# RWKV attention and SwiGLU block: scores and state products of a late unit in two shared banks, VectorE's small work handed out singly, one set of DMAs begun by ScalarE

## The chip, the core and the metric

The kernel runs on one core of one Trainium2 chip. The metric is the time of one execution in device microseconds (us); for the kernel before the change it is 601.09 us, the median of three runs (599.85 to 602.52). The engines are named as in the profile: PE is TensorE's matmul, PEld its weight load, DVE is VectorE, ACT is ScalarE, POOL is GpSimd, SP is the queue of SyncE, which only issues DMAs. A suffix q (SPq, ACTq) is the sequencer of an engine: it waits and issues, and the engine does no arithmetic in that time.

## The reference

An attention block with a decaying state (4 batches, 8 heads, 768 positions, head size 48) is followed by a gated feed-forward block over its 3072 rows of 384 numbers (inner size 1536). All is fp32.

```python
for t in range(S):                       # r, k, v: (4, 8, 768, 48); w, u: (8, 48)
    kt, vt, rt = (k[:, :, t], v[:, :, t], r[:, :, t])
    cur = np.einsum('bhd,bhe->bhde', u[None] * kt, vt)
    y[:, :, t] = np.einsum('bhd,bhde->bhe', rt, state + cur)
    state = w[None, :, :, None] * state + np.einsum('bhd,bhe->bhde', kt, vt)
x = y.transpose(0, 2, 1, 3).reshape(3072, 384)
g = x @ w_gate                           # (3072, 1536)
out = (g / (1 + np.exp(-g)) * (x @ w_val)) @ w_out
```

## The kernel before the change

**Units and steps.** Attention is cut into 24 units, and a loop over steps s = 4 ... 25 works on several units at once: in step s the kernel scales and loads for units s + 1 to s + 3, turns r and k of unit s, computes the scores of unit s - 1 and the outputs of unit s - 2. Units 0 to 11 hold 128 positions of one batch. Units 12 to 23 (those from `PAIRED` = 12 on, the late units) hold 64 positions of each of two batches, one on partitions 0 to 63 and one on 64 to 127; the index `p` names the half. All of the change is in the late units.

**One late unit.** For unit i these parts follow each other:
- `diagonal` (L376, ACT): eight small activations (one for each head) write the diagonal u·k·r terms into `own`, which lies in the tile `zs`. They are not issued at once but put into the queue `small`.
- `fill` (L503 and L504, SP): four DMAs fill the unit's coefficient tile `At`: two bring r from `rT`, two bring the diagonals from `zs`. `At` exists twice, and units take turns.
- `paired_scores` (L516, PE): 32 matmuls of `rT` and `kT` into two banks.
- `masked_copy` (L524, DVE): four predicated copies take the strictly causal scores out of these banks into `At`. Of the four, two are issued at once and two are put into the queue `lazy`.
- `paired_outputs` (L550, PE, then L554, ACT): 64 matmuls of `At` with v and the state (both in `v_ld`) into one bank, and ACT copies it into `xT`, the input of the feed-forward part.
- `paired_update` (L567, PE; L585, DVE; L589, POOL): 32 matmuls form k·v for the state into two banks, four DVE additions add them to the state in `v_ld`, two POOL multiplications apply the decay.

**Banks.** PSUM (the matmuls' output memory) has eight banks here. Four (`bank`) serve the feed-forward matmuls; a bank must be emptied (evicted) by ACT or DVE before the matmuls of a later piece may write it. The other four (`ring`) go round through `next_psum`: each call takes the next. One late step takes one for the outputs, two for the scores and two for the state products: five of a ring of four, so that the last state bank of a step is the bank in which the outputs of the same step lie.

**Pieces.** The feed-forward matmuls fill the time between the parts of attention. They lie in the list `todo` as pieces of one or a few matmul groups each. `feed(n, pops)` issues n pieces, and after each it takes one item of `lazy` and up to `pops` items of `small`. `gaps(s, n)` calls it at five places of a step; `turn_blocks` calls it once between its two DVE transposes (L456). The pieces that matter are of two kinds: in one (`three_beside`, L922) each bank is evicted by DVE additions and ACT copies (L946), followed by the silu (L953, ACT) and its product; in the other (`project`, L738) the sums of h (L711 to L715, DVE) are needed before the matmuls.

**Order.** Nothing is scheduled automatically: each engine runs its instructions in the order in which the program issues them, and waits on semaphores. In step s from 14 on that order was: `own_sum` and `diagonal(s)`, `gaps(s, 0)`, outputs of s - 2, the rest of `lazy`, scores of s - 1, two masked copies, state products, additions and multiplications of s - 2, loads of v, `gaps(s, 1)`, `turn_blocks(s)`, moves for the next turn (L435, SP), `gaps(s, 2)`, the rest of `small`, `fill(s)`, `gaps(s, 3)`, `gaps(s, 4)`. Steps 14 to 16 have 14 pieces each, steps 18 to 20, 22 and 23 have 10, step 17 has 4 and step 21 has 6.

**After the loop** the last four groups of the feed-forward part run by themselves (L922, L1151); the change leaves them as they are.

Of the kernel before, what the change touches and what calls it, by code (L numbers as in the profile page):

```python
# [15 lines left out]
P = 128  # L16
# [6 lines left out]
def fast(  # L23
# [474 lines left out]
    def fill(i):  # L498

        rT = turned[i][:].rearrange("p a (e t) -> p (a e) t", e=2)  # L500
        for p in range(2):
            there, here = slice(64 - 64 * p, P - 64 * p), slice(64 * p, 64 * p + 64)
            sp.dma_start(out=both(i)[there, p], in_=rT[there])  # L503
            sp.dma_start(out=both(i)[here, p], in_=own[here, i % 2])  # L504

    def paired_scores(i, ps):

        rT = turned.pop(i)[:].rearrange("p a (e t) -> p (a e) t", e=2)
        kt = kT[i % 2][:].rearrange("p a (e t) -> p (a e) t", e=2)
        ps = [x.rearrange("p a (e t) -> p (a e) t", e=2)[:, 0:HP] for x in ps]  # L510
# [18 lines left out]
        lazy.popleft()()  # L529
        lazy.popleft()()  # L530
# [25 lines left out]
    def paired_update(i):  # L556

        if i + 2 >= N:
            return
        ps = [next_psum(HP, D) for _ in range(2)]  # L560
        for n in range(HP):
            for p in range(2):
                rows = slice(64 * p, 64 * p + 64)
                for g in range(2):
# [6 lines left out]
                    )  # L571
        for p in range(2):
            o = 64 - 64 * p

            def state(a):
                x = v_ld[part(i, p)[0]][o : o + D, a, 0:1]
                return bass.AP(
                    tensor=x.tensor, offset=x.offset,
                    ap=[list(x.ap[0]), [VW, a.stop - a.start], [64, 2], [1, D]],
                )  # L580

            for g in range(2):
                x = 64 * (1 - (p ^ g))
                ze = state(slice(HP // 2 * g, HP // 2 * g + HP // 2))
                dve.tensor_add(  # L585
                    ze, ps[p][x : x + D].rearrange("p (a e) d -> p a e d", e=2), ze
                )
            ze = state(slice(0, HP))
            pool.tensor_mul(ze, ze, w64[o : o + D].unsqueeze(3).to_broadcast([D, HP, 2, D]))  # L589
# [33 lines left out]
    def update(i):  # L623
        if i >= PAIRED:
            paired_update(i)
            return
# [671 lines left out]
    def gaps(s, n):  # L1298

        if s not in EARLY:  # L1300
# [5 lines left out]
            feed(share[0] // 5 + (n < share[0] % 5) - (n == 1 and BLOCKS <= s < N))  # L1306
# [100 lines left out]
    for s in range(4, N + 2):  # L1407
# [31 lines left out]
        if 4 <= s - 1 < N:  # L1439
            if s <= PAIRED:  # L1440
                flush()
            if s - 2 >= PAIRED:
                outputs(s - 2)
            scores(s - 1)
            if LATE <= s < PAIRED + 2:
                outputs(s - 2)
            if s >= LATE:
                update(s - 2)
            if PAIRED <= s < N:
                load_v(s)  # L1450
            gaps(s, 1)
        if BLOCKS <= s < N:
            turn_blocks(s)
        if late:
# [17 lines left out]
        elif s < N:  # L1472
            flush()
            fill(s)
# [446 lines left out]
```

## Time and profile before

| | |
|---|---|
| median of three runs | 601.09 us |
| the profiled execution, its own time | 598.33 us |
| its span, first to last instruction | 596.6 us |
| TensorE clock granted | 0.998 of full speed |
| matmuls (PE) busy | 575.0 us, 5370 instructions |
| outputs L550, 768 matmuls | 13.3 us |
| scores L516, 384 matmuls | 8.3 us |
| state products L567, 320 matmuls | 8.5 us |
| diagonals L376, 96 activations | 29.0 us, 343 ns each |
| decay L589, 20 POOL multiplications | 16.5 us, 825 ns each |
| DMA At<-rT, 24 of 128 KB | median 2.7 us from issue to landing |
| DMA At<-zs, 24 of 128 KB | median 2.5 us from issue to landing |

The late units' parts run from about 157 us (first masked copy) to about 432 us (last outputs); the tail follows. A row of the timeline has the start, the length, the engine, the line, the operation, what it writes and reads, how many instructions are merged in it, and in square brackets how long the engine sat idle before it and what ended that. A row of the waits has the waiting engine and its line, the engine and line it waited for, and then the total in us, the number of times and the longest.

### The profile page before, as it was taken

How to read it: one execution, taken by the hardware profiler on the slowest of the kernel's cores; microseconds unless marked ns; L12 is line 12 of the kernel's file. 1: busy time of each engine (PE TensorE's matmuls, PEld its weight loads, DVE VectorE, ACT ScalarE, POOL GpSimd, SP SyncE). 2: the span in 40 equal slices, each digit the busy share in tenths (PEclk: the TensorE clock that was granted, in tenths of full speed). 3: DMA queues.
4: the chain of work that ended last, by engine and by line, in shares of the span. 5: the costliest groups of instructions: out<-in, count | busy, mean ns of one | idle time of the engine just before them, and what ended most of it. 6: DMA issues, size and time to landing. Idle time of an engine off the chain costs nothing.

```text
span 596.6 us, 13553 instructions
## 1 busy us (share of the span) xinstructions
PE 575.0 (96%) x5370; PEld 514.7 (86%) x5370; DVE 440.7 (74%) x761; ACT 223.4 (37%) x529; POOL 361.0 (61%) x382
## 2 busy tenths in 40 slices
PE   8999999999999999998989989999999999999996
PEld 7788888899887889987889978889988899888896
DVE  7977777488689695678888578879457878377672
ACT  4658885331244422335321334521034320243410
POOL 6888888999999314887511987424678960011610
PEclk9999999999999999999999999999999999999999
DMA  7999967733652504435354254301100000200002
GB/s 192 234 246 241 302 193 78 102 61 68 131 93 34 101 16 96 80 80 91 49 103 96 59 96 86 71 15 36 42 14 1 0 2 1 54 0 1 1 3 56
DMA packets 151733, 48.08 MB, mean 81 GB/s; under 512 B 139313, under 2 KB 142386, under 8 KB 151666
## 3 DMA queue, kind: packets, MB, share of 16 engines
q1 hardware_dynamic: 148338, 42.85, 34.4%
q10 hardware_dynamic: 3328, 4.33, 2.4%
q8 instruction: 43, 0.70, 0.5%
q14 instruction: 24, 0.20, 0.1%
HBM read 28.31 MB, written 4.72 MB: 55 GB/s over the span
## 4 chain that ended last, share of the span: by engine, by line
PE 75%; DVE 10%; POOL 5%; DMA 3%; issue 2%; ACT 2%; ACTq 1%; SPq 1%; DVEq 0%; POOLq 0%
PE bank L922 22%; PE bank L738 12%; PE ring L922 12%; PE bank L663 10%; PE bank L1151 8%; DVE hv L946 4%; PE ring L617 2%; PE ring L550 2%; POOL wgv L825 2%; POOL s L852 2%; DMA v_ld<-in_v_dram 2%; PE ring L473 1%; PE ring L405 1%; PE ring L1151 1%; DVE At L524 1%
## 5 line engine op out<-in xcount | busy, mean ns | idle before, releaser
L946 DVE TENSOR_TENSOR hv<-hv,bank 128x512 f32<-128x512 f32 x132 | 86.8, 683 | 23.3 <-ACT hv L946 11.8
L922 PE MATMUL bank<-xf,wgv 128*128 128x256 f32 x256 | 66.3, 383 | 1.9 <-DVE hv L946 1.9
L663 PE MATMUL bank<-xT,wgv 128*128 128x256 f32 x288 | 66.3, 384 | 0.0
L946 ACT COPY hv<-bank 128x512 f32<-128x512 f32 x72 | 40.0, 584 | 61.9 <-PE bank L922 53.2
L663 PEld LDWEIGHTS bank<-xT,wgv 128*128 128x128 f32 x288 | 53.5, 190 | 7.9
L852 POOL TENSOR_TENSOR s<-wgv 128x256 f32<-128x256 f32 x39 | 29.8, 786 | 48.1 <-PE bank L738 48.1
L922 PEld LDWEIGHTS bank<-xf,wgv 128*128 128x128 f32 x256 | 47.7, 190 | 9.7 <-DVE hv L946 3.1
L1205 POOL TENSOR_TENSOR hv<-At,hats 128x512 f32<-128x512 f32 x8 | 10.2, 1275 | 66.7 <-ACT At L1204 66.7
L589 POOL TENSOR_TENSOR v_ld<-v_ld,w 48x384 f32<-48x384 f32 x20 | 16.5, 825 | 45.5 <-DVE v_ld L585 27.7
L953 ACT ACTIVATE hv<-hv 128x512 f32<-128x512 f32 (+1 forms) x33 | 21.4, 668 | 57.1 <-DVE hv L946 57.0
L922 PE MATMUL bank<-xT,s 128*128 128x256 f32 x152 | 36.0, 382 | 2.1 <-DVE hv L946 1.1
L922 PE MATMUL bank<-xT,wgv 128*128 128x256 f32 x144 | 35.9, 382 | 0.0
L738 PE MATMUL bank<-wt,hs 128*128 128x192 f32 x192 | 33.7, 328 | 1.6 <-DVE hs L712 1.6
L922 PEld LDWEIGHTS bank<-xT,s 128*128 128x128 f32 x152 | 28.5, 190 | 7.6 <-issue 2.0
L738 PE MATMUL bank<-wo,hs 128*128 128x192 f32 x192 | 33.9, 327 | 0.3 <-DVE hv L746 0.3
L738 PE MATMUL bank<-wo,hv 128*128 128x192 f32 x192 | 33.4, 327 | 0.0
L738 PEld LDWEIGHTS bank<-wt,hs 128*128 128x128 f32 x192 | 31.3, 190 | 2.3 <-DVE hs L712 1.3
L524 DVE COPY_PREDICATED At<-mask,ring 64x256 f32<-64x256 int32 x48 | 21.3, 443 | 15.9 <-PE ring L516 10.4
L376 ACT ACTIVATE zs<-mask,du 128x64 f32<-128x64 f32 x96 | 29.0, 343 | 9.1 <-DVE hv L751 4.1
L738 PEld LDWEIGHTS bank<-wo,hs 128*128 128x128 f32 x192 | 31.6, 190 | 0.8 <-DVE hv L746 0.6
L738 PEld LDWEIGHTS bank<-wo,hv 128*128 128x128 f32 x192 | 31.6, 190 | 0.4
L852 POOL TENSOR_TENSOR s<-s 128x256 f32<-128x256 f32 x39 | 30.6, 784 | 0.9
(239 smaller groups left out, 1427.6 us busy)
## 6 DMA issues: line engine op xcount, KB each, us to landing
hats<-hats SPq DMA_DIRECT2D x96, 64.0 KB, 2.3
w_bits<-in_moe_w_gate_dram SPq DMA_DIRECT2D x6, 768.0 KB, 6.1
w_bits<-in_moe_w_val_dram SPq DMA_DIRECT2D x6, 768.0 KB, 6.1
w_bits<-in_moe_w_out_dram SPq DMA_DIRECT2D x6, 768.0 KB, 7.0
At<-rT SPq DMA_DIRECT2D x24, 128.0 KB, 2.7
At<-zs SPq DMA_DIRECT2D x24, 128.0 KB, 2.5
v_ld<-in_v_dram SPq DMA_DIRECT2D x24, 96.0 KB, 5.5
k_ld<-in_k_dram SPq DMA_DIRECT2D x24, 96.0 KB, 3.1
```

The lines of the kernel that those rows point to most:

```text
L376: lambda h=h: act.activation(own[:, i % 2, slot(i, h), :], ident64, AF.Identity, scale=du[:, h : h + 1])
L524: dve.copy_predicated(both(i)[rows, p, HP * g : HP * g + HP], m, ps[p][o : o + 64])
L550: pe.matmul(ps[32 * q : 32 * q + 32, cc, 64 * p : 64 * p + 64], *x, start=start, stop=stop, skip_group_check=True,)
L589: pool.tensor_mul(ze, ze, w64[o : o + D].unsqueeze(3).to_broadcast([D, HP, 2, D]))
L617: pe.matmul(ps[32 * q : 32 * q + 32, cc, :], *x, start=start, stop=stop, skip_group_check=True,)
L663: pe.matmul(gv[:, o, :].rearrange("p (i t) -> p i t", i=2), wt[:, c, P * f : P * (f + 1)], xT[:, 2 * g % NX : 2 * g % NX + 2, c, :], start ...
L738: pe.matmul(ps, lhs[:, f, :], rhs[:, f, :], start=(f == 0 and n in (0, 1, 4)), stop=(f == FH - 1), skip_group_check=True,)
L852: op(made[o], made[a], made[b])
L922: pe.matmul(ps[:, o], u[:, o], v, start=first and o == 0, stop=True, skip_group_check=True,)
L946: do(out, *(pair_of(wide[a][:]) if isinstance(a, str) else a for a in args))
L953: todo.append((at, lambda: act.activation(gate, gate, AF.Silu)))
L1151: pe.matmul(ps, (h[what][q] if h[what] is D_ else h[what][:, q])[:, f, :], wide["o"][what][:, f, :], start=first and f == 0 and (split or ...
```

## The change

It does five things to the late units.

1. The state products of unit i - 1 are computed inside `paired_scores(i)`, right behind its 32 score matmuls, and go to columns 256 to 447 of the two banks whose columns 0 to 255 hold the scores, with the two banks exchanged. `paired_update` no longer takes banks of its own; a late step takes three banks of the ring instead of five.
2. All four masked copies and all four state additions (the decay behind every second one) go into `lazy`: one of these eight after each piece. What is left is issued at the top of the next step's attention part, ahead of the outputs instead of ahead of the scores.
3. From step 12 on up to three diagonals instead of one follow each piece, and the rest is issued ahead of the outputs, in all steps.
4. `fill` is split. `fill_own`, the two DMAs of the diagonals, is issued by ACT, right behind the copy of the outputs.
5. `fill_turned`, the two DMAs of r, stays on SP, but right behind `turn_blocks`: ahead of the moves (L435), of one gap and of the next loads.

```diff
     def scores(i):
-        while lazy:
-            lazy.popleft()()
         ps = [next_psum(HP, P) for _ in range(2)]
...
-    def fill(i):
+    def fill_turned(i):
         rT = turned[i][:].rearrange("p a (e t) -> p (a e) t", e=2)
         for p in range(2):
-            there, here = slice(64 - 64 * p, P - 64 * p), slice(64 * p, 64 * p + 64)
+            there = slice(64 - 64 * p, P - 64 * p)
             sp.dma_start(out=both(i)[there, p], in_=rT[there])
-            sp.dma_start(out=both(i)[here, p], in_=own[here, i % 2])
+    def fill_own(i):
+        for p in range(2):
+            here = slice(64 * p, 64 * p + 64)
+            act.dma_start(out=both(i)[here, p], in_=own[here, i % 2])
...
     def paired_scores(i, ps):
...
+        sums = [
+            x.rearrange("p a t -> p (a t)")[:, 256 : 256 + HP * D]
+            .rearrange("p (h d) -> p h d", h=HP) for x in reversed(ps)
+        ]
...
                 lazy.append(lambda p=p, g=g: masked_copy(p, g))
-        lazy.popleft()()
-        lazy.popleft()()
+        if PAIRED < i < N - 1:
+            paired_update(i - 1, sums)
...
-    def paired_update(i):
-        if i + 2 >= N:
-            return
-        ps = [next_psum(HP, D) for _ in range(2)]
+    def paired_update(i, ps):
...
+        def add(p, g):
+            x = 64 * (1 - (p ^ g))
+            ze = state(p, slice(HP // 2 * g, HP // 2 * g + HP // 2))
+            dve.tensor_add(ze, ps[p][x : x + D].rearrange("p (a e) d -> p a e d", e=2), ze)
+            if g:
+                ze, w = state(p, slice(0, HP)), w64[64 - 64 * p : 64 - 64 * p + D]
+                pool.tensor_mul(ze, ze, w.unsqueeze(3).to_broadcast([D, HP, 2, D]))
         for p in range(2):
-            o = 64 - 64 * p
...
+            for g in range(2):
+                lazy.append(lambda p=p, g=g: add(p, g))
...
-            feed(share[0] // 5 + (n < share[0] % 5) - (n == 1 and BLOCKS <= s < N))
+            feed(
+                share[0] // 5 + (n < share[0] % 5) - (n == 1 and BLOCKS <= s < N),
+                3 if s >= PAIRED else 1,
+            )
...
         if 4 <= s - 1 < N:
-            if s <= PAIRED:
-                flush()
+            flush()
+            while lazy:
+                lazy.popleft()()
             if s - 2 >= PAIRED:
                 outputs(s - 2)
+                if s < N:
+                    fill_own(s)
             scores(s - 1)
             if LATE <= s < PAIRED + 2:
                 outputs(s - 2)
-            if s >= LATE:
                 update(s - 2)
+                fill_own(s)
...
         if BLOCKS <= s < N:
             turn_blocks(s)
+        if PAIRED <= s < N:
+            fill_turned(s)
...
         if s < PAIRED:
             diagonal(s)
-        elif s < N:
-            flush()
-            fill(s)
```

**Order on PE in step 19.** The rows of the program of before, from the last output matmuls of unit 17 over the scores of unit 18 (ring_97, ring_98) and the state products of unit 17 (L567) to the next piece:

```order
L550 MATMUL ring_96<-At_111,v_ld_108 32x64 x4
L516 MATMUL ring_97<-rT,kT_112 64x64 x2
L516 MATMUL ring_98<-rT,kT_112 64x64 x2
...
L567 MATMUL ring_99<-v_ld_107,hats 64x48 x2
L567 MATMUL ring_96<-v_ld_108,hats 64x48 x2
...
L738 MATMUL bank_93<-wo,hv 128x192 x6
```

The second row of state products writes ring_96, the bank of the outputs that ACT has still to copy. The same place after the change (L557 are the outputs, L523 the scores, L571 the state products, L740 the next piece):

```order
L557 MATMUL ring_98<-At_111,v_ld_108 32x64 x4
L523 MATMUL ring_99<-rT,kT_112 64x64 x2
L523 MATMUL ring_96<-rT,kT_112 64x64 x2
...
L571 MATMUL ring_96<-v_ld_107,hats 64x48 x2
L571 MATMUL ring_99<-v_ld_108,hats 64x48 x2
...
L740 MATMUL bank_93<-wo,hv 128x192 x6
```

The state products now write the banks of the scores, and ring_98 with the outputs is not touched again in this step. The order of the work is the same.

**Order on DVE in step 17.** Before, from the masked copies of unit 16 on:

```order
L524 COPY_PREDICATED At_110<-mask,ring_99 64x256 x2
L585 TENSOR_TENSOR v_ld_107<-ring_97,v_ld_107 48x2x2x48 x2
L585 TENSOR_TENSOR v_ld_108<-ring_98,v_ld_108 48x2x2x48 x2
L456 STREAM_TRANSPOSE kT_113<-hats 128x512
L946 TENSOR_TENSOR hv<-hv,bank_93 128x2x256
L946 TENSOR_TENSOR hv<-bank_95,hv 128x2x256
L524 COPY_PREDICATED At_110<-mask,ring_96 64x256
L456 STREAM_TRANSPOSE rT<-hats 128x512
L946 TENSOR_TENSOR hv<-hv,bank_92 128x2x256
L946 TENSOR_TENSOR hv<-hv,bank_94 128x2x256 x2
L524 COPY_PREDICATED At_110<-mask,ring_96 64x256
```

After, from the same transpose of kT to the end of what is left in `lazy`, in step 18 (L948 are the evictions, L531 the masked copies, L587 the additions):

```order
L456 STREAM_TRANSPOSE kT_113<-hats 128x512
L948 TENSOR_TENSOR hv<-hv,bank_93 128x2x256
L948 TENSOR_TENSOR hv<-bank_95,hv 128x2x256
L531 COPY_PREDICATED At_110<-mask,ring_97 64x256
L456 STREAM_TRANSPOSE rT<-hats 128x512
...
L948 TENSOR_TENSOR hv<-hv,bank_92 128x2x256
L531 COPY_PREDICATED At_110<-mask,ring_98 64x256
L948 TENSOR_TENSOR hv<-hv,bank_93 128x2x256
L948 TENSOR_TENSOR hv<-hv 128x2x256
L587 TENSOR_TENSOR v_ld_107<-ring_98,v_ld_107 48x2x2x48 x2
L587 TENSOR_TENSOR v_ld_108<-ring_97,v_ld_108 48x2x2x48 x2
```

Two copies and four additions that stood ahead of the evictions of bank_93, bank_95 and bank_92 stand behind them. Step 17 has too few pieces for eight items, so the four additions come in one row in step 18, ahead of its outputs.

**Order on ACT from the outputs of step 17 into step 18.** Before (L376 are the diagonals, L554 copies the outputs, L946 evicts, L953 is the silu):

```order
L376 ACTIVATE zs<-mask,du 128x64
L554 COPY xT<-ring_98 128x384
L953 ACTIVATE hv<-hv 128x2x256
L376 ACTIVATE zs<-mask,du 128x64
L946 COPY hv<-bank_93 128x2x256
L953 ACTIVATE hv<-hv 128x2x256 x2
L376 ACTIVATE zs<-mask,du 128x64 x6
L946 COPY hv<-bank_95 128x2x256
L946 COPY hv<-bank_92 128x2x256
```

After, the same place (L507 are the DMAs of `fill_own`, L561 copies the outputs, L948 evicts, L955 is the silu):

```order
L376 ACTIVATE zs<-mask,du 128x64 x8
L561 COPY xT<-ring_96 128x384
L507 DMA At_111<-zs 64x512 x2
L955 ACTIVATE hv<-hv 128x2x256
L948 COPY hv<-bank_93 128x2x256
L955 ACTIVATE hv<-hv 128x2x256 x2
L948 COPY hv<-bank_95 128x2x256
L948 COPY hv<-bank_92 128x2x256
```

All eight diagonals stand ahead of the copy of the outputs, the two DMAs right behind it, and the six diagonals between the silu and the evictions are gone.

More of the change, by code (lines that the diff above doesn't have):

```diff
@@ L571, in paired_update, with state @@
                     )
-        for p in range(2):
-            o = 64 - 64 * p
[L575 to L580, printed above, removed]
-            for g in range(2):
[L583 to L589, printed above, removed]
+        def state(p, a):
+            x = v_ld[part(i, p)[0]][64 - 64 * p : 64 - 64 * p + D, a, 0:1]
+            return bass.AP(
+                tensor=x.tensor, offset=x.offset,
+                ap=[list(x.ap[0]), [VW, a.stop - a.start], [64, 2], [1, D]],
+            )
[6 more added lines that the diff above has]
+                pool.tensor_mul(ze, ze, w.unsqueeze(3).to_broadcast([D, HP, 2, D]))
+        for p in range(2):
+            for g in range(2):
+                lazy.append(lambda p=p, g=g: add(p, g))
     def outputs(i):
@@ L623, in update @@
     def update(i):
-        if i >= PAIRED:
-            paired_update(i)
-            return
         c, b = divmod(i, B)
@@ L1305, in gaps @@
                     share[0] = -(-(len(todo) + (14 if s < 21 else 0)) // max(25 - s, 1))
-            feed(share[0] // 5 + (n < share[0] % 5) - (n == 1 and BLOCKS <= s < N))
+            feed(
+                share[0] // 5 + (n < share[0] % 5) - (n == 1 and BLOCKS <= s < N),
+                3 if s >= PAIRED else 1,
+            )
             return
```

## The prediction

> **What bounds the kernel now.** I read the page first: which engine is full.
>
> ```profile
> span 596.6 us, 13553 instructions
> ...
> PE 575.0 (96%) x5370; PEld 514.7 (86%) x5370; DVE 440.7 (74%) x761; ACT 223.4 (37%) x529; POOL 361.0 (61%) x382
> ```
>
> Matmuls fill 96% of the span. The change removes no matmul, so it can only win time in which PE stands still: at most 596.6 - 575.0 = 21.6 us, start included. Next, three stretches by their windows: up to the first late outputs, the late units, the tail (each row: engine, busy us, in brackets the instructions).
>
> ```profile
> 0.00:172.00 172.00, 167.51 (x1840) 147.53 (x1841) 131.68 (x247) 93.42 (x237) 149.94 (x159) 1.00 0.71 164
> 172.00:432.00 260.00, 249.22 (x2572) 223.01 (x2570) 201.25 (x340) 84.33 (x206) 147.34 (x173) 1.00 0.35 69
> 432.00:597.00 165.00, 158.31 (x964) 144.17 (x960) 107.76 (x175) 45.64 (x87) 63.70 (x52) 0.99 0.05 12
> ```
>
> The columns are PE, PEld, DVE, ACT, POOL. The change touches the middle stretch alone. PE stands still there for 260.00 - 249.22 = 10.8 us, and DVE has 201 us of work in 260. So **10.8 us bounds the gain**. The waits of PE in that stretch say for whom it stands:
>
> ```profile
> PE bank L922 <- DVE hv L946: 3.0, 4, 1.6
> PE bank L922 <- ACT hv L946: 2.9, 3, 1.8
> PE ring L567 <- ACT xT L554: 2.8, 2, 1.7
> PE bank L738 <- DVE hs L712: 1.6, 2, 1.0
> PE bank L738 <- DVE hv L746: 0.3, 1, 0.3
> ```
>
> 12 waits, 10.6 us. Which of them the change reaches, the timeline around each tells.
>
> **Part 1: shared banks.** The third row are state products that wait for ACT to copy the outputs, since both have one bank (steps 19 and 23):
>
> ```profile
> 306.51 0.84 ACT L953 ACTIVATE hv<-hv 128x768 f32<-128x768 f32 x1 [3.08 <-DVE hv L946]
> 307.49 0.46 ACT L554 COPY xT<-ring 128x384 f32<-128x384 f32 x1
> 308.00 0.67 PE L567 MATMUL ring<-v_ld,hats 64*64 64x48 f32 x28 [1.69 <-ACT xT L554]
> 394.12 0.67 PE L567 MATMUL ring<-v_ld,hats 64*64 64x48 f32 x28 [1.14 <-ACT xT L554]
> ```
>
> ACT was stuck behind a silu that waits for DVE. After the change the products write the banks of the scores, which PE has just had; the copy stays as late as it was, but its bank is next written a step later, and nobody else in the step waits for it. **-2.8 us**, the surest term. What is late next are the pieces behind: their first groups need only h that is long there, so PE goes on.
>
> **Part 2: the DMAs and the burst on DVE, step 21.**
>
> ```profile
> 349.29 0.54 SPq L504 DMA_DIRECT2D At<-zs  x1
> 349.45 0.81 PE L567 MATMUL ring<-v_ld,hats 64*64 64x48 f32 x32
> 351.71 0.90 DVE L524 COPY_PREDICATED At<-mask,ring 64x256 f32<-64x256 int32 x2 [3.03 <-DMA At<-zs]
> 352.62 1.48 DVE L585 TENSOR_TENSOR v_ld<-ring,v_ld 48x192 f32<-48x192 f32 x4
> 354.75 1.88 DVE L946 TENSOR_TENSOR hv<-hv,bank 128x512 f32<-128x512 f32 x3
> 355.49 1.13 PE L922 MATMUL bank<-xf,wgv 128*128 128x256 f32 x4 [1.59 <-DVE hv L946]
> 358.06 1.13 PE L922 MATMUL bank<-xf,s 128*128 128x256 f32 x4 [0.57 <-ACT hv L946]
> ```
>
> SP was late with the diagonals, because loads and moves stood ahead of them on its queue. DVE waits 3.03 us for them, copies twice, adds four times, and only then evicts; PE has run out of banks. After the change ACT issues the diagonals in step 20 right behind the copy of the outputs, SP the other half before the moves: over 10 us earlier than they are read. The copies and sums stand behind the evictions. Both waits go: **-2.2 us**.
>
> **Part 3: diagonals and burst, step 17** (first the window around it, then rows of the timeline).
>
> ```profile
> 264.00:277.00 13.00, 10.92 (x166) 8.85 (x166) 12.05 (x22) 6.14 (x16) 10.21 (x12) 1.00 0.47 77
> ...
> 266.11 0.89 DVE L524 COPY_PREDICATED At<-mask,ring 64x256 f32<-64x256 int32 x2 [0.15 <-PE ring L516]
> 267.01 1.48 DVE L585 TENSOR_TENSOR v_ld<-ring,v_ld 48x192 f32<-48x192 f32 x4
> 272.41 1.13 PE L922 MATMUL bank<-xf,wgv 128*128 128x256 f32 x4 [0.31 <-DVE hv L946]
> 274.12 1.53 ACT L376 ACTIVATE zs<-mask,du 128x64 f32<-128x64 f32 x6
> 276.16 1.13 PE L922 MATMUL bank<-xf,s 128*128 128x256 f32 x4 [1.76 <-ACT hv L946]
> ```
>
> Six diagonals in one row (1.53 us) hold up the eviction that PE waits for, behind a DVE that is 0.89 + 1.48 = 2.37 us late from its own burst. By the new order neither stands there. **-2.1 us** (0.31 + 1.76).
>
> **Part 4: the burst elsewhere.** The other waits, steps 14, 15, 18, 22 and 23:
>
> ```profile
> 186.47 1.97 PE L922 MATMUL bank<-xT,s 128*128 128x256 f32 x8 [0.79 <-DVE hv L946]
> 217.13 2.22 PE L738 MATMUL bank<-wt,hs 128*128 128x192 f32 x12 [1.02 <-DVE hs L712]
> 292.83 0.92 PE L922 MATMUL bank<-xf,s 128*128 128x256 f32 x3 [0.57 <-ACT hv L946]
> 376.29 1.97 PE L922 MATMUL bank<-xT,s 128*128 128x256 f32 x8 [0.28 <-DVE hv L946]
> 407.44 1.86 PE L738 MATMUL bank<-wt,hs 128*128 128x192 f32 x10 [0.56 <-DVE hs L712]
> ```
>
> With the 0.3 us of L746 they are 3.5 us. In each, DVE has run without a break since the burst, which is up to 2.37 us of work ahead of what PE waits for; behind it, the wait could go whole. But the work is moved and not removed, and these stretches are the dense ones. Between nothing and 3.5 us I take **-2.5 us**, nearer to the upper end, since in each the moved work is longer than the wait.
>
> **What it adds.** First, the sums left over. Step 17 has so few pieces that four additions fall into step 18, ahead of its scores, and one of the score banks is the one that the last two of them read:
>
> ```profile
> 280.28 0.69 DVE L946 TENSOR_TENSOR hv<-hv 128x512 f32<-128x512 f32 x1
> 280.86 0.69 PE L516 MATMUL ring<-rT,kT 48*64 48x64 f32 x32
> 366.47 0.69 DVE L946 TENSOR_TENSOR hv<-bank,hv 128x512 f32<-128x512 f32 x1 [0.17 <-PE bank L922]
> 367.40 0.69 PE L516 MATMUL ring<-rT,kT 48*64 48x64 f32 x32
> ```
>
> DVE is through with its last eviction at 280.97; four additions (1.48 us, above) end at 282.4, and the third score matmul, due at 280.95, waits for them: **+1.45 us**. In step 22 two are left: 367.16 + 0.74 = 367.9 against 367.45, **+0.45 us**. Second, the eight items handed out:
>
> ```profile
> L946 DVE TENSOR_TENSOR hv<-hv,bank 128x512 f32<-128x512 f32 x118 | 77.5, 683 | 20.5 <-ACT hv L946 11.1 <-PE bank L922 8.2
> L524 DVE COPY_PREDICATED At<-mask,ring x48: 425/444/456, 157.6 to 420.1; 64x256 f32<-64x256 int32 x48
> L585 DVE TENSOR_TENSOR v_ld<-ring,v_ld x40: 348/354/363, 177.0 to 395.9; 48x192 f32<-48x192 f32 x40
> L762 ACTq DMA_DIRECT2D out_dram<-hv x20: 338/368/609, 139.0 to 431.9; - x20
> ```
>
> Each puts 0.35 or 0.44 us ahead of an eviction, where DVE has idled 20.5 / 118 = 0.17 us on average. Mostly a second bank is free and PE doesn't notice. The 40 additions and the 22 copies that were in a burst are 14.2 + 9.8 = 24 us; PE could see none of it, or at the worst all. The nearest rows are PE's seven waits at L922 of before, when 22 copies already came singly: most of the seven are put down to bursts above. I take one item in sixteen as seen by PE, four at 0.4 us: **+1.5 us**. Third, ACT pays two DMA issues a unit, 0.37 us each by its own stores: 12 x 0.74 = 8.9 us. They stand behind the copy of the outputs, where ACT idles (84 us busy in 260), and the copy waits for the same matmuls as they do, so they add no wait: nothing here, 0.74 us a step if an eviction were due at once. The diagonals come earlier in a step in threes, 0.5 us more ahead of two evictions, hidden by the same idle time. POOL's multiplications come later; the state is read two steps on.
>
> **The sum.** -2.8 - 2.2 - 2.1 - 2.5 + 1.45 + 0.45 + 1.5 = **-6.2 us** on the profiled execution's 598.33 us (span 596.6 plus 1.7 around it), so 592.1. The median of the runs is 601.09, 2.8 above it; the difference carries over: 601.1 - 6.2 = **594.9**, said as 595.0.
>
> **A rule to weigh.** PE's writes of the sums and DVE's reads of the scores now share a bank. In the rows above the products take 0.81 us right behind the scores. If DVE had to keep off the bank for them, ten units would lose at most 8.1 us, and the sum would be +1.9: 600.2 on this execution, 603 in the median. By the new order an eviction of the next piece, whose matmuls come behind the products, stands between them in all steps but 17 and 21, and there a transpose does; so I give it nothing in the sum. The Trainium skill, "PSUM — Partial Sum Buffer", Terms, has such a rule: TensorE's write and VectorE's read of one bank and quadrant at a time collide, so that the two have to be kept apart. No run here shows a case of it.
>
> **Rivals.** (1) *The waits move on*: only the two of part 1 and part 2's DMA wait go for good, and where DVE was dense, PE, now earlier, meets the same DVE a little later. For it: DVE has 12.05 us of work in the 13 us of the window in part 3. The sum is then -2.8 - 2.2 + 1.9 + 1.5 = -1.6: 599.5. Chance 0.24. (2) *The spread items become the bound*, the slower side: more than 10.8 / 0.4 = 27 of the 62 moved items reach PE, each holding a bank. If all did and all else were gained, 24 + 1.9 - 9.6 = +16; if half did, +4: 605. Against it: DVE is 77% busy in the stretch. Chance 0.06. (3) *The shared bank* as above, 603: 0.04. (4) *The gain is lost in the tail*: PE reaches 432 earlier, but POOL's weight sums are no earlier: no change, 601. Against it: POOL has 64 us of work in the tail's 165. Chance 0.04. The forecast has the other 0.62.
>
> **Range and chances.** All 10.8 gained and only the 1.9 paid is -8.9: 592.2, with the runs' own spread of 1.3 us 591.0. Upwards it takes in rival 1: 600.5. Some 0.5% (3 us) is about what a measurement of this kernel can tell from no change. Faster by more: the forecast and a third of rival 1, 0.70; within: 0.21; slower: rivals 2 and 3 less their mild cases, 0.09.
>
> **What would show it.** No wait of the state products for xT; no wait of DVE for At<-zs; DVE's sums one by one; a new wait of the scores for the state additions at about 280 and 367; PE idle between 172 and the last late outputs down from 10.8 to 4 or 5 us, the stretch some 6 us shorter, the tail as long as before. I am wrong if PE stands behind evictions at new places for more than 4 us in all, or if the tail grows.

## The result, and the profile after

| | before | after |
|---|---|---|
| median in the first comparison | 600.63 us (4 runs) | 593.15 us (591.23 to 594.88, 4 runs) |
| ratio to before, 95% interval | 1 | 0.987 (0.9831 to 0.9909) |
| the profiled execution, its own time | 598.33 us | 592.9 us |
| its span | 596.6 us | 591.1 us |
| median in the experiments | 598.53 us (11 runs) | 593.11 us (6 runs), ratio 0.9916 (0.989 to 0.9942) |

The kernel is faster by 7.5 us in the first comparison and by 5.4 in the second; the two intervals overlap. The forecast gain of 6.2 us lies between the two. The forecast time, 595.0 us, is 1.9 above the measured one: it starts from a median of 601.09 us, while the kernel before had medians of 598.53, 598.61 and 599.37 in the experiments.

The page of the kernel after begins like this:

```profile
span 591.1 us, 13539 instructions
...
PE 572.7 (97%) x5370; PEld 513.3 (87%) x5370; DVE 443.8 (75%) x761; ACT 223.2 (38%) x529; POOL 364.3 (62%) x382
```

The three stretches by their windows (PE, PEld, DVE, ACT, POOL, then clock, DMA share and GB/s; the window is cut at 426, the last late outputs end at 426.8):

```profile
0.00:172.00 172.00, 166.38 (x1842) 146.66 (x1843) 130.91 (x248) 94.23 (x239) 150.53 (x159) 1.00 0.71 166
172.00:426.00 254.00, 247.21 (x2526) 222.02 (x2528) 205.02 (x339) 83.17 (x204) 149.40 (x173) 0.99 0.35 69
426.00:592.00 166.00, 159.09 (x1018) 144.65 (x1007) 107.89 (x176) 45.76 (x87) 64.41 (x52) 0.99 0.05 13
```

Counted from 172 to the end of the last late outputs, the stretch of the late units went from 260.0 to 254.8 us, 5.2 shorter; the tail kept its length (164.6 and 164.3 us). PE stands still in the late stretch for 254.00 - 247.21 = 6.8 us, where it was 10.8. The waits of PE tell for whom (waiting engine, releaser, total us, times, longest):

```profile
PE bank L924 <- ACT hv L948: 2.6, 1, 2.6
PE ring L523 <- DVE v_ld L587: 2.4, 2, 1.7
...
PE bank L924 <- DVE hv L948: 0.8, 2, 0.6
...
PE bank L924 <- POOL s L854: 0.4, 1, 0.4
```

Of the 12 waits that the prediction listed (10.6 us), one of 0.39 us is left, at 185 (the fourth row). No state product waits for xT, and no masked copy waits for At<-zs. The second row is the new wait that was forecast, the scores for sums left over. The third row (0.59 us at 361, 0.18 at 190) is at new places. The first row was not forecast. The first two rows make up 5.0 of the 6.8 us, so the experiments had two questions: which part of the change took the old waits away, and where the 2.6 us come from.

### The profile page after: what moved, and what is told of

It reads as the page before. It is cut to its first block, busy times and chain, and to the rows that moved or that the text cites. A ratio compares the mean times of both kernels' runs of the same rounds, so it can differ in the third digit from the quotient of the medians.

```text
span 591.1 us, 13539 instructions
## 1 busy us (share of the span) xinstructions
PE 572.7 (97%) x5370; PEld 513.3 (87%) x5370; DVE 443.8 (75%) x761; ACT 223.2 (38%) x529; POOL 364.3 (62%) x382
## 4 chain that ended last, share of the span: by engine, by line
PE 75%; POOL 10%; DVE 7%; SPq 2%; issue 2%; ACT 1%; DMA 1%; ACTq 1%; DVEq 0%; POOLq 0%
PE bank L924 23%; PE ring L924 12%; PE bank L740 12%; PE bank L665 11%; PE bank L1153 8%; POOL s L854 4%; POOL wgv L827 3%; DVE hv L948 3%; PE ring L622 2%; PE ring L557 2%; PE ring L471 1%; PE ring L1153 1%; PE ring L523 1%; PE ring L405 1%; SPq L153 1%
## 5 line engine op out<-in xcount | busy, mean ns | idle before, releaser
L948 DVE TENSOR_TENSOR hv<-hv,bank 128x512 f32<-128x512 f32 x132 | 86.6, 683 | 33.7 <-PE bank L924 25.8
L590 POOL TENSOR_TENSOR v_ld<-v_ld,w 48x384 f32<-48x384 f32 x20 | 19.3, 965 | 76.8 <-DVE v_ld L587 75.1
L948 ACT COPY hv<-bank 128x512 f32<-128x512 f32 x72 | 40.3, 588 | 68.3 <-PE bank L924 52.3
L665 PEld LDWEIGHTS bank<-xT,wgv 128*128 128x128 f32 x288 | 53.4, 190 | 8.0
L955 ACT ACTIVATE hv<-hv 128x512 f32<-128x512 f32 (+1 forms) x33 | 21.2, 669 | 51.2 <-DVE hv L948 48.8
L740 PE MATMUL bank<-wo,hs 128*128 128x192 f32 x192 | 34.0, 327 | 0.3 <-DVE hv L756 0.2
L740 PE MATMUL bank<-wt,hs 128*128 128x192 f32 x192 | 33.7, 328 | 0.1
L740 PE MATMUL bank<-wo,hv 128*128 128x192 f32 x192 | 33.4, 327 | 0.0
L740 PEld LDWEIGHTS bank<-wo,hs 128*128 128x128 f32 x192 | 31.6, 190 | 1.1 <-DVE hv L756 0.4
L740 PEld LDWEIGHTS bank<-wt,hs 128*128 128x128 f32 x192 | 31.3, 190 | 0.7 <-issue 0.6
L740 PEld LDWEIGHTS bank<-wo,hv 128*128 128x128 f32 x192 | 31.6, 190 | 0.4
L854 POOL TENSOR_TENSOR s<-s,wgv 128x256 f32<-128x256 f32 x39 | 29.7, 761 | 2.5
L924 PEld LDWEIGHTS bank<-xT,wgv 128*128 128x128 f32 x144 | 26.7, 190 | 5.0 <-DVE hv L948 1.6
```

Of the source, the lines that this page charges most:

```text
L590: pool.tensor_mul(ze, ze, w.unsqueeze(3).to_broadcast([D, HP, 2, D]))
L665: pe.matmul(gv[:, o, :].rearrange("p (i t) -> p i t", i=2), wt[:, c, P * f : P * (f + 1)], xT[:, 2 * g % NX : 2 * g % NX + 2, c, :], start ...
L740: pe.matmul(ps, lhs[:, f, :], rhs[:, f, :], start=(f == 0 and n in (0, 1, 4)), stop=(f == FH - 1), skip_group_check=True,)
L854: op(made[o], made[a], made[b])
L924: pe.matmul(ps[:, o], u[:, o], v, start=first and o == 0, stop=True, skip_group_check=True,)
L948: do(out, *(pair_of(wide[a][:]) if isinstance(a, str) else a for a in args))
```

## Experiments: the parts of the change alone and in pairs

For this the change is cut into three: **banks** (its part 1), **single** (part 2, copies and sums one by one) and **fills** (parts 3 to 5, diagonals in threes and the DMAs). The kernels ran in three groups (e1 to e4, e5 to e8, e9 to e12), each on a chip of its own with runs of the kernel before beside it, so the ratios are what is compared.

| kernel | median us | ratio to before (95%) |
|---|---|---|
| banks alone, copies ahead of the products (e1_banks) | 606.19 | 1.0129 (1.0109 to 1.015) |
| banks alone, products first (e5_banks_first) | 597.7 | 0.9982 (0.9966 to 0.9998) |
| single alone (e2_single) | 604.02 | 1.0082 (1.0051 to 1.0113) |
| fills alone (e6_fills) | 600.16 | 1.0036 (1.0014 to 1.0057) |
| banks + single (e7_nofills) | 594.32 | 0.9927 (0.9906 to 0.9949) |
| single + fills (e9_ownbanks) | 603.05 | 1.0064 (1.004 to 1.0088) |
| banks + fills (e10_burst) | 594.82 | 0.9929 (0.9905 to 0.9953) |
| all three, the change (e4_again) | 593.11 | 0.9916 (0.989 to 0.9942) |

**Banks alone.** To the kernel before:

```diff
     def paired_scores(i, ps):
+        sums = [... [:, 256 : 256 + HP * D] ... for x in reversed(ps)]
...
         lazy.popleft()()
         lazy.popleft()()
+        if PAIRED < i < N - 1:
+            paired_update(i - 1, sums)
```

> The kernel before with the shared banks alone: the state products go to columns 256 to 447 of the score banks; masked copies, sums, diagonals and DMAs stay as before. By the prediction's part 1: the two waits of the state products for xT (1.69 and 1.14 us) are gone, the burst of step 21 and the diagonals of step 17 stay: 2.8 us faster than before, ratio 0.995. By the first rival (the waits move on): PE arrives earlier at the same bursts and waits there instead: at most 1 us faster. By the rival of the colliding bank: slower by up to 8 us, with products that take visibly longer than 0.81 us.

It was 1.3% slower, 7.7 us. The rival of the colliding bank had allowed up to 8 us, but by products that take longer; these take what they took before, and it is PE that waits ahead of them. The waits of PE in this kernel (L570 are the state products, L528 the masked copies):

```profile
PE ring L570 <- DVE At L528: 12.2, 10, 2.9
```

In each of ten units the products wait for the two masked copies issued just ahead of them. The copies read columns 0 to 255 and the products write 256 to 447, but in this kernel the writer of a shared bank waits for its earlier reader all the same. So the experiment had measured the order of the code in a shared bank, and not the bank alone. The second try issues the products first, as the change does (`paired_update` then issues the matmuls and returns the sums, which are run after the copies):

```diff
+        add = paired_update(i - 1, sums) if PAIRED < i < N - 1 else None
         lazy.popleft()()
         lazy.popleft()()
-        if PAIRED < i < N - 1:
-            paired_update(i - 1, sums)
+        if add:
+            add()
```

> The kernel before with the shared banks alone, as in e1_banks, but with the state products issued ahead of the first two masked copies, as the change has it; copies and sums are issued at once behind the products. Theory: in e1_banks PE waited ten times for the masked copies that stand ahead of the products in a shared bank, which is a matter of the order and not of the bank; without it the 2.8 us of the prediction's part 1 show: 0.995 of before, and no wait of the products at all. Rival: the products and the copies collide in the bank, or the copies now wait for the products (0.81 us) and DVE's burst is late by that much ten times: no gain, or up to 8 us slower.

Now the products wait for nothing, and the kernel gains 0.9 us of the 2.8 expected (by the ratio 1.1). The same window of both kernels, first before and then this one:

```profile
172.00:430.00 258.00, 247.22 (x2503) 221.37 (x2502) 200.89 (x339) 84.33 (x206) 145.34 (x172) 1.00 0.35 69
```

```profile
172.00:430.00 258.00, 246.67 (x2516) 219.28 (x2519) 198.33 (x339) 84.08 (x205) 146.24 (x172) 1.00 0.35 69
```

PE's idle time has not fallen at all, 11.3 us against 10.8. The two waits for xT are gone, but PE waits 1.83 us at 217 for the sums of h (1.02 before) and at four new places (183, 286, 373 and 396) for some 0.5 us each. Taken alone, this part went the way of the first rival: the waits moved on. One source of them is the bank after all, as this experiment's own rival had it: the copies now wait for the products, and not for the scores alone. DVE's waits, before and then in this kernel:

```profile
DVE At L524 <- PE ring L516: 10.4, 9, 2.9
```

```profile
DVE At L528 <- PE ring L571: 14.1, 8, 3.4
```

So DVE's bursts begin about half a microsecond later behind PE's scores. How much of PE's new waits is due to that, and how much to PE's being earlier, no run separates. What the part does gain is another thing: the 32 products take 0.63 us instead of 0.81 where they follow the scores in the scores' banks, in all ten units.

**Single alone.** To the kernel before (`add` as in the change; what is left in `lazy` still goes out behind the outputs, ahead of the scores):

```diff
             for g in range(2):
                 lazy.append(lambda p=p, g=g: masked_copy(p, g))
-        lazy.popleft()()
-        lazy.popleft()()
...
         for p in range(2):
             for g in range(2):
-                ...
-                dve.tensor_add(...)
+                lazy.append(lambda p=p, g=g: add(p, g))
```

> The kernel before with the small work of DVE handed out singly, and nothing else: four masked copies and four sums go out one after each piece; the state products keep banks of their own, the diagonals and all DMAs stay as before. By the prediction: part 4 and half of part 3 are gained (2.5 + 1 us), the waits for xT (2.8) and for the DMA At<-zs (2.2) stay, leftover sums ahead of the scores cost 1.9 and single items 1.5: no change within 1 us. By the first rival (dense DVE): nothing is gained and the 3.4 us are paid: 603 to 604. If handing out is the larger part of the whole gain: 3 us faster or more.

Slower by about 5 us, more than either theory. PE waits 4.2 us for xT (3.06 at the longest), 2.60 us at 200 as in the change, and the granted clock of its six runs was 0.984 to 0.996, where before had 0.995 to 1.0: behind long waits PE ran slowly for some us (see the last section).

**Fills alone.** To the kernel before: `fill_own` behind the copy of the outputs, `fill_turned` behind `turn_blocks`, three diagonals a piece and `flush()` ahead of the outputs, all as in the change.

> The kernel before with parts 3 to 5 of the change alone: three diagonals a piece and the rest ahead of the outputs, diagonals' DMAs by ACT behind the copy of the outputs, r's DMAs by SP behind the turn. Banks, copies and sums as before. By the prediction: DVE no longer waits 3.03 us for At<-zs in step 21 and the diagonals of step 17 are out of the way, but the bursts stay: 2 to 3 us faster, ratio 0.995 to 0.997. By the first rival: each wait that goes is found again a little later, within 0.5 us of before.

DVE's wait for At<-zs went, and the wait at 276 fell from 1.76 to 0.34 us. The kernel was nevertheless 0.4% slower, which neither theory had. Its waits of PE show the price (L572 are the state products):

```profile
PE ring L572 <- ACT xT L559: 7.1, 7, 2.6
```

Before, it was 2 waits and 2.8 us. The rest of the diagonals now stands ahead of ACT's copy of the outputs, and the bank that the state products want is the one that this copy empties. Behind the longest of these waits, 2.64 us, the granted clock was at about 0.5 for some 6 us besides. The pairs show what hides it.

**Without the banks** (the change, but `paired_update` takes two banks of its own behind the scores, as before):

> The changed kernel without its part 1: the state products have two banks of their own again, copies and sums go out singly, diagonals and DMAs as in the change. Theory: parts 3 to 5 put the rest of the diagonals ahead of ACT's copy of the outputs, and with own banks the state products wait for that copy (in e6_fills 6 times, 6.9 us); shared banks are what hides it. So without them the waits for xT come back at more than the 4.2 us of e2_single, and the kernel is slower than before: 603 to 607. Rival: single items and early DMAs are the gain and the banks matter little: 594 to 596.

As the theory had it. In the timeline at step 19, first of this kernel, the copy L555 comes behind a silu (L955) and five diagonals (L376), and the products (L568) wait for it:

```profile
308.61 0.84 ACT L955 ACTIVATE hv<-hv 128x768 f32<-128x768 f32 x1 [3.98 <-DVE hv L948]
309.36 1.29 ACT L376 ACTIVATE zs<-mask,du 128x64 f32<-128x64 f32 x5
310.55 0.46 ACT L555 COPY xT<-ring 128x384 f32<-128x384 f32 x1
311.06 1.09 PE L568 MATMUL ring<-v_ld,hats 64*64 64x48 f32 x28 [4.02 <-ACT xT L555]
```

The five diagonals are 1.29 us of this. The silu is late as well: DVE's product ahead of it took 2.33 us behind a row of POOL's operations, instead of 0.95 before (see the next section). In the kernel after, the same copy (L561) is as late and nobody waits:

```profile
306.83 0.63 PE L571 MATMUL ring<-v_ld,hats 64*64 64x48 f32 x32
307.40 1.89 PE L740 MATMUL bank<-wo,hv 128*128 128x192 f32 x10
308.68 0.84 ACT L955 ACTIVATE hv<-hv 128x768 f32<-128x768 f32 x1 [3.98 <-DVE hv L948]
309.43 1.29 ACT L376 ACTIVATE zs<-mask,du 128x64 f32<-128x64 f32 x5
310.62 0.46 ACT L561 COPY xT<-ring 128x384 f32<-128x384 f32 x1
```

**Without the fills** (diagonals, their DMAs and r's as before):

> The changed kernel without its parts 3 to 5 (diagonals, their DMAs and r's as before), so shared banks and single items alone. If the DMAs matter as part 2 says: DVE waits for At<-zs again in step 21 (about 3 us), and now a masked copy handed out between evictions holds up the evictions behind it: 2 to 4 us slower than the changed kernel. If they don't: the same as the changed kernel (593.1).

The same as the change within the intervals, and DVE does not wait for At<-zs although SP issues these DMAs at the old place. The copies, handed out one by one, come after the DMA has landed. Of the long waits of before only that for the diagonals of step 17 is left in part, 1.08 us at 277.

**Without the single items** (two copies and the four sums at once behind the products):

```diff
+        add = paired_update(i - 1, sums) if PAIRED < i < N - 1 else None
+        lazy.popleft()()
+        lazy.popleft()()
+        if add:
+            for p in range(2):
+                for g in range(2):
+                    add(p, g)
```

> The changed kernel without its part 2: shared banks with the products ahead of the copies, two copies and the four sums issued at once behind them, diagonals and DMAs as in the change. Theory: the banks hide what parts 3 to 5 cost in e6_fills, the waits of the steps 17 and 21 for diagonals and DMA are gone, those for bursts stay, and nothing is left over ahead of the scores: 594.5 to 596. Rival: the parts add up as they measured alone (-0.9 and +1.6): 599.3.

594.82, as the theory had it: of the long waits of the steps 17 and 21 (1.76 and 1.59) 0.34 and 0.24 us are left, and with the bursts eleven other waits of 0.2 to 0.8 us at evictions and 1.83 us at 217 stay.

What follows from the table: alone, the three parts sum up to 0.0082 + 0.0036 - 0.0018 = 1.0% slower; together they are 0.84% faster. The shared banks are what makes the other two pay: out of the whole they are worth (1.0064 - 0.9916) x 599 = 8.9 us, alone 0.9. With them, either of the other parts brings 3 us more, and the second of them another 0.7, which is within the intervals. How much of the 8.9 would be left with the decay moved (next section), no run tells.

## Experiments: the two new waits

**The leftover sums.** The changed kernel with two small items a piece where a step has fewer than eight pieces:

```diff
-            if lazy:
+            for _ in range(min(2 if 0 < share[0] < 8 else 1, len(lazy))):
                 lazy.popleft()()
```

The rows that it is aimed at, timeline of the kernel after at step 18:

```profile
278.51 1.02 DVE L948 TENSOR_TENSOR hv<-hv 128x512 f32<-128x512 f32 x1
279.55 1.48 DVE L587 TENSOR_TENSOR v_ld<-ring,v_ld 48x192 f32<-48x192 f32 x4
281.08 0.62 PE L523 MATMUL ring<-rT,kT 48*64 48x64 f32 x26 [1.66 <-DVE v_ld L587]
...
282.56 2.07 PE L924 MATMUL bank<-xf,wgv 128*128 128x256 f32 x4
284.43 1.32 PE L924 MATMUL bank<-sgs,s 128*128 128x256 f32 x4
285.58 1.03 PE L924 MATMUL bank<-sgs,wgv 128*128 128x256 f32 x4
```

Four sums in a row (1.48 us) stand ahead of the scores, which wait 1.66 us for them, and the first matmuls behind take 2.07 us for four instead of 1.03.

> The changed kernel, but where a step has fewer than eight pieces (13, 17 and 21) two small items follow each piece instead of one, so that no sum is left over ahead of the scores of steps 18 and 22. Theory: the leftover sums alone make the scores wait (1.66 us in step 18, 0.73 in step 22), and those waits go; the doubled items cost 0.4 us at two or three evictions: 1.5 to 2.5 us faster than the changed kernel, about 591.3 where it has 593.2. Rival: in the steps with few pieces DVE is dense, and two items at once hold up evictions as the bursts before did: within 0.5 us of the changed kernel, with new waits of PE at L924 in the steps 17 and 21.

591.9 us, ratio 0.9879 (0.9859 to 0.9899): 1.2 us under the changed kernel by the medians, 2.2 by the ratios, at the edge of what the intervals tell apart. The waits did as expected: 0.52 us in step 18 instead of 1.66, none in step 22 instead of 0.73, and one of 0.52 at an eviction in step 17.

**The changed kernel again.**

> The changed kernel once more, on the chip of the other runs, as their measure. Both theories: 593.2 us, 7.5 less than before. Open is what of its profile comes back: if the wait of 2.60 us at 200.78 (PE for an eviction by ACT, behind a product on DVE that took 3.99 us) stands in this profile too, it belongs to the order of the program; if not, to chance. The same for the granted clock, which fell in one slice behind the wait of the scores at 281.

The wait came back, 2.60 us at 200.36. All seven profiles of kernels with single items and the decay at its place have it, 2.59 or 2.60 us at 200 to 201; the kernels with bursts (before, e1, e5, e6, e10) do not. In the timeline of the kernel after:

```profile
195.73 0.82 POOL L590 TENSOR_TENSOR v_ld<-v_ld,w 48x384 f32<-48x384 f32 x1 [1.26 <-PE bank L924]
195.97 3.99 DVE L948 TENSOR_TENSOR hv<-hv 128x512 f32<-128x512 f32 x1 [0.39 <-ACT hv L955]
196.51 0.99 POOL L353 TENSOR_TENSOR hats<-k_ld,scales 128x384 f32<-128x384 f32 x1
197.47 0.99 POOL L356 TENSOR_TENSOR hats<-r_ld,scales 128x384 f32<-128x384 f32 x1
198.43 0.99 POOL L264 TENSOR_TENSOR rk<-r_ld,k_ld 128x384 f32<-128x384 f32 x1
199.49 1.33 POOL L267 TENSOR_TENSOR rk<-rk,scales 128x384 f32<-128x384 f32 x1
200.05 0.59 ACT L948 COPY hv<-bank 128x512 f32<-128x512 f32 x1 [3.12 <-DVE hv L948]
200.78 2.83 PE L924 MATMUL bank<-xT,s 128*128 128x256 f32 x12 [2.60 <-ACT hv L948]
```

A product of two SBUF operands on DVE, 0.69 us where nothing is in its way, takes 3.99 us while POOL runs four operations without a gap. ACT waits for the product, PE for ACT. In the kernel before the same product took 1.48 us, at 196.58. The decay (L590), moved behind a sum that is now handed out late (it ends on DVE at 195.58), stands at the head of POOL's row and lets it begin late: POOL's waits in the kernel after, and then in e11_decay_only (L591 and L588 there):

```profile
POOL v_ld L590 <- DVE v_ld L587: 75.1, 8, 26.1
```

```profile
POOL v_ld L591 <- DVE v_ld L588: 13.3, 5, 3.5
```

POOL does not stand idle less for that: in e11 it waits longer at other work (56.4 us at L855 for PE, 7.5 in the kernel after). What counts is what stands behind the head.

**The decay moved.** In e11 this is the only edit to the changed kernel; e8 is e3 with the same edit. The decays go into a queue of their own, which is emptied behind `own_product(s + 1)` and ahead of the outputs:

```diff
-                pool.tensor_mul(ze, ze, w.unsqueeze(3).to_broadcast([D, HP, 2, D]))
+                decays.append(lambda: pool.tensor_mul(ze, ze, ...))
...
             own_product(s + 1)
+            while decays:
+                decays.popleft()()
```

> The changed kernel with the one edit of e8_decay (POOL's decay multiplications behind the next step's scalings) but one small item a piece everywhere. Theory: the wait of 2.60 us at 200 goes, with the slow clock behind it (1.3 us), and the waits of the scores for the leftover sums stay at 281 and 364: 589.5 to 590.5. Rival: the gain of e8_decay belongs to both edits together, since the shifted steps meet other waits: 592 or more.

> The kernel of e3_two with one more edit: POOL's decay multiplications wait until behind the next step's scalings on POOL. Theory: the wait of 2.60 us at 200 comes from a product of two SBUF operands on DVE (3.99 us instead of 0.69) that cannot run while POOL does four operations without a gap, the decay and three of the next step; without the decay at their head POOL's row begins sooner and ends sooner, DVE's product takes about 2 us and PE's wait falls from 2.6 to under 1 us: 590 or a little less, and 1.5 us more where the clock no longer falls behind it. Rival: the three scalings alone hold DVE as long: 591.9 as e3_two.

e11: 590.74 us, 0.9853 (0.9826 to 0.988), just above what its theory had; the wait at 200 is gone, and those for the leftover sums stay (1.66 and 0.73 us). e8: **588.92 us, 0.9833 (0.9815 to 0.9851)**, the fastest kernel of the study, 10 us under before. Timeline of e8 at the same place (L949 is the product, L925 the matmuls):

```profile
193.96 1.00 POOL L353 TENSOR_TENSOR hats<-k_ld,scales 128x384 f32<-128x384 f32 x1
194.92 1.00 POOL L356 TENSOR_TENSOR hats<-r_ld,scales 128x384 f32<-128x384 f32 x1
195.66 0.81 DVE L949 TENSOR_TENSOR hv<-hv 128x512 f32<-128x512 f32 x1 [0.39 <-ACT hv L956]
195.89 1.45 POOL L264 TENSOR_TENSOR rk<-r_ld,k_ld 128x384 f32<-128x384 f32 x1
197.72 2.75 PE L925 MATMUL bank<-xT,s 128*128 128x256 f32 x12
```

POOL's scalings begin 2.5 us earlier (L353 at 193.96 instead of 196.51). The product takes 0.81 us instead of the 2 that were expected, here POOL's L264 is the one that is stretched (1.45 us), and PE waits for nothing. A wait of 1.09 us for POOL at 274 is new in e8. That the order on POOL is the cause is shown by the edit; why DVE got in behind POOL's second operation here and behind the third after the decay there, no run shows.

**The issuer of the diagonals' DMAs.** The changed kernel with `sp.dma_start` instead of `act.dma_start` in `fill_own`:

> The changed kernel with the DMAs of the diagonals issued by SP instead of ACT, at the same place in the program. By the prediction: ACT's issues (0.545 us each as measured, 24 of them) lie in its idle time, so nothing changes: 593.1 within 0.6 us. Rival: behind two issues an eviction or a copy of ACT starts up to 1.1 us late, PE sees some of it: 1 to 2 us faster without them. Other rival: SP waits at these DMAs for the diagonals, the loads behind them are late: slower by 1 us or more.

592.78 us, 0.9895 (0.9865 to 0.9925): no difference from the change that can be measured.

## Why the prediction was right, point by point

- **Bound.** PE's idle time in the late stretch bounded the gain, 10.8 us, and the tail kept its length. Right. The sum said 4 to 5 us left; 6.8 were left. The prediction's sign of being wrong, more than 4 us behind evictions at new places, was nearly reached: 3.5 (2.60, 0.59, 0.18 and 0.15).
- **Part 1, banks (-2.8).** Both waits went. The step that failed is "the copy stays as late as it was": in step 19 ACT's copy of the outputs now begins at 310.62, 4.2 us behind the last output matmul (before, 1.9). About 1 us of that is the diagonals flushed ahead of the outputs, which stand in front of it; 1.4 is the silu's wait for a DVE product held up by POOL (2.33 us instead of 0.95; with the decay moved, in e11, it takes 0.95 again and the copy begins 2.9 us behind). It cost nothing for the reason given there, that its bank is not written in that step. The term was right for the sum and wrong for the part: the banks also cover some 6 us that the other parts would have cost (e6, e9).
- **Part 2 (-2.2).** The waits of 1.59 and 0.57 us went, but not by the earlier DMAs alone: without them (e7) the DMA wait stays away too, since the copies come later, and with bursts (e10) the early DMAs suffice.
- **Part 3 (-2.1).** Gone. Here both halves count: 1.76 becomes 1.08 with single items (e2, and with banks e7), 0.34 with the diagonals spread (e6, and with banks e10), and nothing with both.
- **Part 4 (-2.5 of 3.5).** Of these waits, 0.39 us is left at 185 (now for POOL). Better than taken, by some 0.6 us.
- **Leftover sums (+1.45, +0.45).** 1.66 and 0.73 us, at the two places named. The mechanism was right, and the size short by the clock: behind the longer wait PE lost another 1.6 us in the profile (last section), which no term held.
- **Single items (+1.5).** Without the 0.39 us just counted, 6.8 - 2.6 - 2.4 - 0.4 = 1.4 us of PE's idle time are left, of which 0.92 are waits at new places. The size was about right; that the items cause all of it is not shown.
- **"POOL's multiplications come later; the state is read two steps on": taken at nothing.** This is the step that failed. The state was in time, but POOL works in order: the late decay held its row up and pushed it under a product of DVE. By e11 against e4 it costs (0.9916 - 0.9853) x 599 = 3.8 us; against e12, the change but for the issuer and in e11's own group, 2.5; by e8 against e3, 2.8. The wait is 2.6 of it. The rest, if there is one, is likely the clock, which fell behind this wait in six of the seven profiles.
- **ACT's DMA issues.** 0.545 us each (median of 24) instead of the 0.37 of the stores; hidden, as said (e12).
- **Rivals.** The shared bank did not slow PE in the change's order, it made it faster: ten times 0.81 - 0.63 = 1.8 us that no term held. Why the products are shorter there, the runs do not settle; with own banks they take 0.81 in most units (e2, e9). The price that this rival feared, up to 8.1 us, does exist in the other order: with the copies ahead of the products the waits made the kernel 7.7 us slower (e1). "The waits move on" holds for the banks alone (e5) and not for the whole.

The sum came out because its misses went both ways. Too little was taken for the new wait (2.6), the clock (1.6) and the leftover sums (0.5), together 4.7 us; too much for the single items (0.1), and too little for the old waits (0.6 us more went) and the products (1.8), together 2.5. -6.2 + 4.7 - 2.5 = -4.0 us, against -5.4 in the profiled execution and -5.4 in the second comparison; the remaining 1.4 us were not traced, and single executions of this kernel lie further apart than that. That the total came so near is luck in good part: misses of 4.7 us one way and of 2.5 the other stand against a forecast of 6.2.

## What to carry to other kernels

Parts of a change are not priced by measuring or summing them alone: here a bank that nobody else wants turned two losing edits into winning ones. When work on one engine is handed out later, what stands behind it in program order on every other engine moves too; look at what each in-order queue has at its head. And in these profiles a wait of PE of some 2.6 us mostly cost about one and a half times its length, by the clock behind it, so the longest one is the one to remove first.

## What the runs showed of the hardware

**The clock behind a wait.** Windows of 2 us of the kernel after behind the wait that ends at 281.08 (third number from the end: granted clock):

```profile
280.00:282.00 2.00, 0.92 (x47) 0.92 (x50) 0.98 (x3) 0.79 (x3) 1.85 (x4) 0.90 0.59 100
282.00:284.00 2.00, 2.00 (x25) 1.64 (x22) 0.00 (x0) 0.00 (x0) 1.29 (x2) 0.50 0.39 95
284.00:286.00 2.00, 2.00 (x8) 1.70 (x7) 0.91 (x2) 0.00 (x0) 0.00 (x0) 0.75 0.43 72
286.00:288.00 2.00, 2.00 (x11) 1.75 (x10) 1.82 (x4) 0.00 (x0) 0.00 (x0) 1.00 0.17 24
```

Half the clock for about 3 us: 0.92 x 0.10 + 2.00 x 0.50 + 2.00 x 0.25 = 1.6 us of matmul time lost. Behind the wait of 4.02 us in e9_ownbanks it lasts longer:

```profile
310.00:312.00 2.00, 0.94 (x28) 0.93 (x28) 2.00 (x4) 1.01 (x4) 0.00 (x0) 0.50 0.63 125
312.00:314.00 2.00, 2.00 (x10) 1.92 (x7) 1.95 (x3) 0.00 (x0) 0.00 (x0) 0.50 0.63 139
314.00:316.00 2.00, 2.00 (x8) 2.00 (x7) 0.00 (x0) 0.00 (x0) 0.00 (x0) 0.50 0.40 70
316.00:318.00 2.00, 2.00 (x12) 2.00 (x12) 0.00 (x0) 0.32 (x1) 0.00 (x0) 0.88 0.00 0
```

In the late stretches of the 14 profiles, 10 of the 11 waits of 2.59 us or more were followed by half the clock, and 2 of the 16 waits between 1.5 and 2.4 us; once, in e2, it came behind two waits of 1.1 and 1.0 us, 6 us apart. So the same wait is punished in one execution and not in the next, and that makes part of the spread of the runs. The Trainium skill, "TensorE: Matmul & The Clock Gate", Part 1, has the half clock, after an idle window of some 3.4 us that runs freely; the 0.50 agrees, but waits shorter than that window were enough here.

**DVE behind a row of POOL.** There are two cases: the product of 3.99 us above, and one of 2.33 us (128x768, 0.95 before) at 305, behind two more of POOL's operations. The Trainium skill, "SBUF — State Buffer", Who interferes with whom, says that a DVE instruction with two SBUF inputs and a GpSimd instruction that reads SBUF exclude each other for an instruction's length. The trace agrees that they do, and shows that the loser can wait through several instructions that follow each other without a gap.
